# Two attention and two gated-unit layers on one core: the order of the work read from a table instead of a planner, and the first loads put on other queues

## The chip, the cores and the metric

The kernel runs on one core of a Trainium2 chip. The core has five engines with queues of their own: TensorE (PE, matrix products; the loads of its stationary operand are shown as PEld), VectorE (DVE), ScalarE (ACT), GpSimd (POOL) and SyncE (SP, which here only issues DMAs). ACT issues some DMAs too. Each engine takes its instructions strictly in the order of the program, and waits at an instruction until the semaphores it names have been set. Matmul results land in PSUM; DVE and ACT bring them to SBUF.

The metric is the device time of one execution in microseconds. Before the change the median of 3 runs is 382.63 us (381.41 to 382.69). The profiled execution took 380.91 us, and its span from the first to the last instruction is 379.2 us.

## The reference

The input is 2048 tokens of 512 numbers in bfloat16. Two kinds of layer alternate, twice: a linear attention A with 32 heads of 16, and a gated unit B of width 1376. Both layers A use the same weights, and so do both layers B.

```python
def _A_ref(x, wqkv, w_phi, wo):
    qkv = split into q, k, v of shape (1, 32, 2048, 16) from x @ wqkv
    pq = jnp.einsum("bhsd,hdf->bhsf", q, w_phi)
    pk = jnp.einsum("bhsd,hdf->bhsf", k, w_phi)
    phi_q = jnp.concatenate([_softmax(pq), _softmax(-pq)], axis=-1)
    phi_k = jnp.concatenate([_softmax(pk), _softmax(-pk)], axis=-1)
    kv = jnp.einsum("bhsf,bhsd->bhfd", phi_k, v)
    z  = jnp.einsum("bhsf->bhf", phi_k)
    num = jnp.einsum("bhqf,bhfd->bhqd", phi_q, kv)
    den = jnp.einsum("bhqf,bhf->bhq", phi_q, z)[..., None] + 1e-6
    return (num / den, heads joined) @ wo

def _B_ref(x, W_gate, W_up, W_down):
    gate, up = x @ W_gate, x @ W_up
    return (gate * (gate > 0) * up) @ W_down

x = x + _A_ref(_layernorm(x), ...)
x = x + _B_ref(_layernorm(x), ...)
x = x + _A_ref(_layernorm(x), ...)
x = x + _B_ref(_layernorm(x), ...)
```

## The kernel before, in words

The 2048 tokens are 16 tiles of 128, in four chunks of four. X stays in SBUF in bfloat16 all the time, and so do all weights, which are loaded once.

**Attention.** Each tile is normalised (`Norm.add`: batch-norm statistics `bnst` on DVE, the power -0.5 on POOL, the scaling on ACT or DVE), then turned so that the 512 features lie on the partitions, either by a DMA transpose on SP's queue or by PE with a copy out of PSUM. The key weights and w_phi are multiplied ahead into one matrix: `feature_weights` turns the key weights on PE (line 351), copies them (ACT or DVE), multiplies with the block form `Wblk` of w_phi (line 364) and copies the product to `Wk`; the same with the query weights to `Wq`. A tile's keys then take one matmul group (line 710), two exponentials on ACT (plus and minus, line 715), the sums of each head on DVE (lines 682 and 692; line 688 where POOL has added two halves, line 679), a reciprocal (724), and the scaling, split between DVE and POOL (730). The product with the values (line 663) is summed over all 16 tiles in PSUM (752). After the last tile `build_R` lays the sums out. Queries go the same way (lines 794, 798, 803 to 814), are turned by a DMA transpose (line 816), and multiplied with R (line 833, "er"). The quotient (851, 853) is turned (860, 866 or 873), multiplied with wo (884) and added to X (566). `Centre` subtracts the mean and turns the tile for the gated unit (524 to 542).

**Gated unit.** `glu` works by chunk, in parts of the chunk (`PARTS`), over ten blocks of 128 columns plus a rest of 96 (line 593). Gate and up products are matmuls with up to 512 tokens wide (613), ACT copies one of them (619, 623), DVE multiplies (626, 630). The down-projection (645) sums eleven blocks per tile; the result is scaled with the square of the norm's factor and added to X (570). In the second layer the tile is stored.

**The order.** Nothing is issued while these functions run: they record operations with an engine, a duration and what they read and write (`Plan.op`). `Plan.order` then plays the program through with these durations. At each moment an idle engine takes, of the operations whose inputs and buffers are there, the one with the highest sum of its longest path to the end and a number of its group (`RANK`); an operation of DVE marked `port` is not begun while a long one of POOL runs. The table `STEP` says for each tile which engine does a step. The resulting order is the order of the instructions on each engine, and also settles which buffer an operation gets. `load_weights` records 28 loads on SP (wo, the rests wr, wg, wu, wd), which the planner puts between SP's transposes. Ahead of all that `setup` issues the first loads: on SP the key weights, tiles 1, 2 and 3 of X and the value weights, on ACT tile 0, w_phi and the rest of X with the query weights. `wake` records matmuls on zeros, which are not used.

Of the kernel before, what the change touches and what calls it, by code (L numbers as in the profile page):

```python
# [8 lines left out]
P = 128  # L9
D = 512  # L10
# [3 lines left out]
NDB = D // P  # L14
# [36 lines left out]
TAIL = {"PE": 0.165, "ACT": 0.12, "DVE": 0.115, "POOL": 0.045, "SP": 0.0}  # L51
SAME = {"PE": -0.165, "ACT": 0.035, "DVE": 0.035, "POOL": 0.08, "SP": 0.0}
HOPS = {("DVE", "POOL"): 0.09, ("ACT", "POOL"): 0.15}
NEXT = {"PE": 0.055, "SP": 0.03}
FREE = 0.06


def hop(a, b):
    return SAME[a] if a == b else HOPS.get((a, b), NEXT.get(b, 0.04))


class Plan:
# [10 lines left out]
    def op(self, eng, occ, fn, reads=(), writes=(), holds=(), lat=0.0, at=0.0, group=None, port=False, long=False):  # L73

        o = Op()
        o.eng, o.occ, o.cost, o.fn, o.lat, o.at, o.port, o.long = eng, occ, occ + TAIL[eng], fn, lat, at, port, long
        o.group, o.i_in = group or self.group
        base, slope = RANK.get(f"{o.group}.{eng}") or RANK[o.group]
        o.bias = base - slope * o.i_in
        o.preds, o.succs, o.i = set(), [], len(self.ops)  # L80
# [18 lines left out]
    def order(self):  # L99
        for o in self.ops:  # L100
            for p in o.preds:
                p.succs.append(o)
        for o in reversed(self.ops):
            o.rank = o.cost + o.lat + max([s.rank + hop(o.eng, s.eng) for s in o.succs], default=0.0)
        free = {k: [0.0] * n for k, (pool, n) in self.kinds.items()}
        engines = sorted({o.eng for o in self.ops})
        busy = {e: 0.0 for e in engines}
        ready = {e: [] for e in engines}
        for o in self.ops:
            o.wait, o.t0 = len(o.preds), o.at  # L110
            if not o.wait:
                ready[o.eng].append(o)
        seq, left, now, shut = [], len(self.ops), 0.0, 0.0
        while left:
            moved, later = False, []
            for e in engines:
                if busy[e] > now + 1e-9:
                    later.append(busy[e])
                    continue
                best = None  # L120
                for o in ready[e]:
                    if o.t0 > now + 1e-9:
                        later.append(o.t0)
                        continue
                    if o.port and shut > now + 1e-9:
                        later.append(shut)
                        continue
                    ok = True
                    need = {}
                    for b in o.bufs:  # L130
                        if b.slot is None:
                            need[b.kind] = need.get(b.kind, 0) + 1
                    for k, n in need.items():
                        got = [t for t in free[k] if t is not None]
                        if len(got) < n:
                            ok = False
                        else:
                            t = sorted(got)[n - 1]
                            if t > now + 1e-9:
                                later.append(t)  # L140
                                ok = False
                    if ok and (best is None or (o.rank + o.bias, -o.i) > (best.rank + best.bias, -best.i)):
                        best = o
                if best is None:
                    continue
                o = best
                ready[e].remove(o)
                moved, left = True, left - 1
                o.start, end = now, now + o.cost
                busy[e] = now + o.occ  # L150
                if o.long:
                    shut = end
                later.append(busy[e])
                for b in o.bufs:
                    if b.slot is None:
                        b.slot = min((i for i, t in enumerate(free[b.kind]) if t is not None),
                                     key=lambda i: free[b.kind][i])
                        free[b.kind][b.slot] = None
                        b.end = 0.0
                    b.left -= 1  # L160
                    b.end = max(b.end, end + o.lat + FREE)
                    if not b.left:
                        free[b.kind][b.slot] = b.end
                for s in o.succs:
                    s.wait -= 1
                    s.t0 = max(s.t0, end + o.lat + hop(e, s.eng))
                    if not s.wait:
                        ready[s.eng].append(s)
                seq.append(o)
            if not moved:  # L170
                later = [t for t in later if t > now + 1e-9]
                assert later, "the plan is stuck"
                now = min(later)
        self.seq = seq
        return seq
# [15 lines left out]
WF_IN, WK_IN, WV_IN, WQ_IN, LOADED = 3.4, 4.2, 6.7, 10.4, 11.0  # L191
X_IN = [3.3, 4.5] + [5.2] * 2 + [7.4] * 4 + [8.9] * 4 + [11.8] * 4
# [8 lines left out]
def setup(ctx, tc, A_x, A_wqkv, A_w_phi, A_wo, B_W_gate, B_W_up, B_W_down, out):  # L201
# [35 lines left out]
    nc.scalar.dma_start(out=X[:, 4:8, :], in_=xv[:, 4:8, :])  # L237
    nc.scalar.dma_start(out=X[:, 8:12, :], in_=xv[:, 8:12, :])
    nc.scalar.dma_start(out=wq[:], in_=wv[:, :, 0:D])
    nc.scalar.dma_start(out=X[:, 12:16, :], in_=xv[:, 12:16, :])  # L240
# [53 lines left out]
def load_weights(st):  # L294

    nc, seen = st.nc, {}
    for n, (name, dst, src, kb) in enumerate(st.loads):
        i = seen[name] = seen.get(name, -1) + 1
        st.pl.rank("ld" if name == "wd" else "l", n)
        st.pl.op("SP", max(0.45, kb / 245.0), lambda dst=dst, src=src: nc.sync.dma_start(out=dst, in_=src), writes=[(name, i)], at=LOADED, lat=2.0)  # L300
# [11 lines left out]
def wake(st):  # L312

    nc, pl = st.nc, st.pl
    pl.rank("z")
    for i in range(STEP["wake"]):
        z = Buf("ps", [P, D], F32)
        pl.op("PE", 0.43 if i < 7 else 0.22, lambda z=z: nc.tensor.matmul(z[:], lhsT=st.zero[:, 0:P], rhs=st.zero[:], start=True, stop=True),
              writes=[(z, 0)], at=1.2)
# [689 lines left out]
```

## Time and profile before

| what | value |
|---|---|
| median of 3 runs | 382.63 us (381.41 to 382.69) |
| the profiled execution | 380.91 us, span 379.2 us |
| PE busy | 363.6 us (96%), 2380 matmuls |
| DVE busy | 268.0 us (71%) |
| ACT busy | 205.5 us (54%) |
| POOL busy | 121.1 us (32%) |
| DMA moved | 32.61 MB, mean 86 GB/s |
| chain that ended last, by engine | PE 64%, DVE 24%, DMA 6% |

The profile shows one execution. A row of a group names the source line, the engine, the operation, what is written and read, how often, the busy time and mean duration, and the idle time of the engine ahead of it with what ended it. Rows in order of time begin with the start and the length in us; "x4" says that four instructions in a row were merged. Matmuls overlap, so their single durations are longer than the distance from one to the next. Instructions that only issue a DMA are shown as SPq or ACTq and do not count as busy; the time a transfer takes runs from the issue to the landing, in the view of DMA issues. "PEclk" is the granted clock of PE.

### The profile page before, as it was taken

What the parts mean: (1) busy time and instruction counts of PE and PEld (TensorE: products, weight loads), DVE (VectorE), ACT (ScalarE), POOL (GpSimd) and SP (SyncE); (2) the same over time, 40 slices, a digit from 0 to 9 for tenths busy, and PEclk for the clock granted to TensorE, in tenths of its full rate; (3) what the DMA queues carried; (4) which work ended last, traced back from release to release, by engine and by line L of the source; (5) the groups of instructions that cost most, each with busy time, mean ns of one, the idle gap of its engine ahead of it and who ended that gap; (6) DMA issues with size and microseconds to landing.
All of it is one profiled execution on the core that took longest, in us unless ns stands there. A gap on an engine that the chain in (4) does not pass through costs nothing.

```text
span 379.2 us, 6724 instructions
## 1 busy us (share of the span) xinstructions
PE 363.6 (96%) x2380; PEld 189.9 (50%) x2409; DVE 268.0 (71%) x608; ACT 205.5 (54%) x439; POOL 121.1 (32%) x203
## 2 busy tenths in 40 slices
PE   4898999999899999999999999999999999999996
PEld 2444545756445444444444456475654445454444
DVE  4999999999925442763497998999962675172433
ACT  4898979776762446737706925865234135514100
POOL 3798965131110220560155681724310002000000
PEclk9999999999999999999999999999999999999999
DMA  8889936788950230021013070478930075000011
GB/s 262 239 143 227 260 44 144 133 149 146 145 107 2 42 58 15 0 30 27 0 22 77 9 119 3 87 127 146 171 85 14 5 146 115 14 0 16 1 55 57
DMA packets 98882, 32.61 MB, mean 86 GB/s; under 512 B 90560, under 2 KB 98336, under 8 KB 98848
## 3 DMA queue, kind: packets, MB, share of 16 engines
q1 hardware_dynamic: 97216, 29.93, 39.7%
q10 hardware_dynamic: 1632, 2.24, 1.8%
q8 instruction: 19, 0.31, 0.4%
q14 instruction: 15, 0.12, 0.1%
HBM read 8.44 MB, written 2.10 MB: 28 GB/s over the span
## 4 chain that ended last, share of the span: by engine, by line
PE 64%; DVE 24%; DMA 6%; issue 2%; ACT 1%; POOL 1%; SPq 0%; POOLq 0%; ACTq 0%
PE ps L613 37%; PE ps L645 14%; PE ps L884 5%; DMA b<-b 4%; DVE sk L682 4%; DVE rk L724 3%; DVE bnst L388 3%; PE ps L794 3%; PE ps L593 3%; DVE sk L692 2%; DVE b L730 2%; PE q L833 2%; DMA X<-in_A_x_dram 2%; DVE sq L682 1%; DVE sk L688 1%
## 5 line engine op out<-in xcount | busy, mean ns | idle before, releaser
L613 PE MATMUL ps<-b,wu 128*128 128x512 bf16 (+2 forms) x400 | 79.2, 336 | 0.6 <-DMA b<-b 0.6
L613 PE MATMUL ps<-b,wg 128*128 128x512 bf16 (+2 forms) x400 | 78.6, 336 | 0.0
L645 PE MATMUL ps<-wd,b 128*128 128x512 bf16 (+3 forms) x368 | 78.1, 366 | 0.3
L623 ACT ACTIVATE b<-ps 128x512 bf16<-128x512 f32 (+2 forms) x100 | 50.5, 520 | 39.6 <-PE ps L613 39.1
L626 DVE SCALAR_TENSOR_TENSOR b<-ps,b 128x512 bf16<-128x512 f32 (+2 forms) x60 | 35.1, 598 | 39.9 <-PE ps L613 38.9
L645 PEld LDWEIGHTS <-b 128*128 128x128 bf16 (+1 forms) x374 | 35.3, 98 | 39.1
L613 PEld LDWEIGHTS <-wg 128*128 128x128 bf16 x400 | 36.1, 98 | 33.1
L613 PEld LDWEIGHTS <-wu 128*128 128x128 bf16 x400 | 36.2, 98 | 32.7 <-issue 0.9
L730 POOL TENSOR_TENSOR b<-b,rk 128x1024 bf16<-128x1024 bf16 (+6 forms) x28 | 37.5, 1351 | 9.6 <-DVE rk L724 7.9
L798 ACT ACTIVATE b<-ps 128x512 bf16<-128x512 f32 x64 | 33.0, 638 | 5.7 <-PE ps L794 5.1
L715 ACT ACTIVATE b<-ps 128x512 bf16<-128x512 f32 x64 | 33.7, 628 | 1.3 <-PE ps L710 1.3
L679 POOL TENSOR_TENSOR b<-b 128x256 f32<-128x256 bf16 x30 | 19.7, 670 | 43.9 <-ACT b L715 34.1
L570 DVE SCALAR_TENSOR_TENSOR X<-ps,r,X 128x512 bf16<-128x512 f32 (+2 forms) x26 | 18.2, 701 | 20.2 <-PE ps L645 20.1
L710 PE MATMUL ps<-Wk,b 128*128 128x512 bf16 x123 | 29.4, 379 | 2.0 <-DMA b<-b 1.2
L884 PE MATMUL ps<-wo,b 128*128 128x512 bf16 x118 | 29.7, 379 | 1.5 <-DMA b<-b 0.9
L630 DVE TENSOR_TENSOR b<-b,b 128x512 bf16<-128x512 bf16 (+2 forms) x40 | 13.5, 348 | 24.0 <-ACT b L623 22.3
L552 POOL TENSOR_SCALAR ve<-tot 128x4 f32<-128x4 f32 x8 | 1.9, 233 | 88.8 <-ACT sq L548 88.8
L663 PE MATMUL ps<-wkv,b 128*128 128x512 bf16 x122 | 29.9, 386 | 0.3
L794 PE MATMUL ps<-Wq,b 128*128 128x512 bf16 x126 | 29.5, 379 | 0.1
L548 ACT ACTIVATE sq<-b 128x512 bf16<-128x512 bf16 x32 | 20.1, 627 | 17.4 <-DVE b L527 17.0
L598 ACT CAST ur<-ps 128x192 bf16<-128x192 f32 (+1 forms) x18 | 5.4, 302 | 32.2 <-PE ps L593 32.1
L814 POOL TENSOR_TENSOR b<-b,rq 128x512 bf16<-128x512 bf16 x19 | 20.2, 1061 | 8.4 <-DVE rq L807 6.1
(94 smaller groups left out, 493.7 us busy)
## 6 DMA issues: line engine op xcount, KB each, us to landing
out_dram<-X SPq DMA_DIRECT2D x15, 128.0 KB, 1.8
X<-in_A_x_dram ACTq DMA_DIRECT2D x3, 512.0 KB, 7.2
b<-b SPq DMA_TRANSPOSE x94, 3.2
wg<-in_B_W_gate_dram SPq DMA_DIRECT2D x8, 160.0 KB, 3.2
wu<-in_B_W_up_dram SPq DMA_DIRECT2D x8, 160.0 KB, 4.0
wd<-in_B_W_down_dram SPq DMA_DIRECT2D x5, 256.0 KB, 4.7
wkv<-in_A_wqkv_dram SPq DMA_DIRECT2D x2, 512.0 KB, 7.1
wq<-in_A_wqkv_dram ACTq DMA_DIRECT2D x1, 512.0 KB, 8.3
```

The source lines that it names most:

```text
L613: nc.tensor.matmul(ps[:], lhsT=wt[:, b, f * P:(f + 1) * P], rhs=xnT[:, lo:hi, b, :], start=(b == 0), stop=(b == NDB - 1))
L623: pl.op("ACT", 0.045 + 0.43 * share, lambda ups=ups, ru=ru, sign=1.0 if fuse else -1.0: nc.scalar.activation(out=ru[:], in_=ups[:], func=A ...
L626: pl.op("DVE", 0.06 + 0.548 * share, lambda gps=gps, ru=ru, h=h, cs=cs: nc.vector.scalar_tensor_tensor(out=h[:, cs], in0=gps[:], scalar=0. ...
L645: nc.tensor.matmul(yps[:], lhsT=hs[f][:fsz, ti * P:(ti + 1) * P], rhs=st.wd[:fsz, f, cols], start=(f == 0), stop=(f == NFT - 1))
L663: nc.tensor.matmul(vp[:], lhsT=xnT[:, ti, kb, :], rhs=st.wkv[:, kb, D:2 * D], start=(kb == 0), stop=(kb == NDB - 1))
L710: nc.tensor.matmul(ps[:], lhsT=xnT[:, ti, kb, :], rhs=w(kb), start=(kb == 0), stop=(kb == NDB - 1))
L715: pl.op("ACT", 0.48, lambda s=s, ek=ek, pk=pk: nc.scalar.activation(out=ek[:, :, s, :], in_=pk[:].rearrange("p (j x) -> p j x", j=8), func ...
L730: eng.tensor_tensor(out=phiK[:, lo:hi, :, :].rearrange("p j s (f h) -> p (j s) f h", h=4), in0=ek[:, lo:hi, :, :].rearrange("p j s (f h) - ...
L794: nc.tensor.matmul(pq[:], lhsT=xnT[:, ti, kb, :], rhs=st.Wq2[:, kb, :], start=(kb == 0), stop=(kb == NDB - 1))
L798: pl.op("ACT", 0.48, lambda s=s, eq=eq, pq=pq: nc.scalar.activation(out=eq[:, :, s, :], in_=pq[:].rearrange("p (j x) -> p j x", j=8), func ...
L814: (nc.vector if on_dve else nc.gpsimd).tensor_tensor(out=e, in0=e, in1=rq[:].unsqueeze(2).to_broadcast([P, 8, DH, 4]), op=Alu.mult)
L884: nc.tensor.matmul(yps[:], lhsT=turned(b), rhs=st.wo[:, b, :], start=(b == 0), stop=(b == NDB - 1))
```

## The change

The planner and the table RANK are gone. A table `ORDER` of 1867 numbers now says directly in which order the recorded operations are issued; `Plan.order` only hands out buffers, of those free at that place the one whose last use lies furthest back. STEP has new entries for almost every tile: which engine copies, sums and scales, which tiles are turned by PE. The first chunk of the first gated unit is cut into three parts (0 to 1, 1 to 2, 2 to 4) instead of two. No norm is made from sums any more (`sA` 0 instead of 2), and the gate that keeps the second layer's queries behind its key sums holds for the last chunk only (`gate` 3 instead of 1). 26 matmuls on zeros are recorded instead of 3, and the table puts them at places where PE has to wait at the start. An alternative path for the first keys (`raw`) is there and not used (`raw` is 0). The durations given with the operations are other ones in places, but nothing reads them now.

The first loads are issued from two lists: on SP tiles 0 and 1 of X and w_phi, on ACT the key weights first, then tiles 2 and 3, the value weights, and the rest, ahead of the load of ACT's function table.

```diff
     def order(self):
-        for o in self.ops:
-            for p in o.preds:
-                p.succs.append(o)
-        for o in reversed(self.ops):
-            o.rank = o.cost + o.lat + max([s.rank + hop(o.eng, s.eng) for s in o.succs], default=0.0)
...
+        owner = {k: [None] * n for k, (pool, n) in self.kinds.items()}
+        last = {k: [-1] * n for k, (pool, n) in self.kinds.items()}
+        assert sorted(ORDER) == list(range(len(self.ops)))
+        self.seq = [self.ops[i] for i in ORDER]
+        for at, o in enumerate(self.seq):
+            o.place = at
+            assert all(hasattr(p, "place") for p in o.preds), "an operation before what it needs"
+            for b in o.bufs:
+                if b.slot is None:
+                    free = [i for i, u in enumerate(owner[b.kind]) if u is None or not u.left]
+                    b.slot = min(free, key=lambda i: last[b.kind][i])
+                    owner[b.kind][b.slot] = b
+            for b in o.bufs:
+                b.left -= 1
+                last[b.kind][b.slot] = at
+        return self.seq
...
+LOAD_SP = ((0, 1), (1, 2), "f")
+LOAD_ACT = ("k", (2, 4), "v", (4, 8), (8, 12), "q", (12, 16))
...
-    nc.sync.dma_start(out=wkv[:, :, 0:D], in_=wv[:, :, D:2 * D])
-    nc.scalar.dma_start(out=X[:, 0:1, :], in_=xv[:, 0:1, :])
-    nc.scalar.dma_start(out=wf[:], in_=A_w_phi.rearrange("(b j) d f -> (j d) b f", b=NDB, j=8))
-    nc.sync.dma_start(out=X[:, 1:2, :], in_=xv[:, 1:2, :])
-    nc.sync.dma_start(out=X[:, 2:4, :], in_=xv[:, 2:4, :])
-    nc.sync.dma_start(out=wkv[:, :, D:2 * D], in_=wv[:, :, 2 * D:3 * D])
...
+    for what in LOAD_SP:
+        load(nc.sync, what)
+    for what in LOAD_ACT:
+        load(nc.scalar, what)
...
-    "part0": "4111", "part1": "6111", "tB0": "D---", "tB1": "--DA", "tA": "----", "wev": "ADADAAAAADDAAAAA",
+    "raw": 0, "kev": "ADAD", "part0": "3111", "part1": "6111", "tB0": "AD--", "tB1": "---A", "tA": "----",
+    "wev": "AAAAAAAADDDAAAAA", "xn1": "ADADDAADDAADAAAA", "turn": "-A--", "wake": 26, "fuse0": "AFAA",
...
+ORDER = [int(i) for i in """
+0 1 2 4 139 135 3 5 149 147 131 8 9 134 126 138 129 140 137 10 11 6 156 151 157 152 150 7 132 12 164 125 153 127 160
...
+""".split()]
```

What that does to the engines' instructions is shown at three places. In these rows, `b` with a number is a working tile, `ps` a PSUM tile, `wkv` the key and value weights, `X` the tokens.

ACT's first instructions, before:

```order
L226 DMA X<-in_A_x_dram 128x512
L227 DMA wf<-in_A_w_phi_dram 128x4x16
L236 ACT_TABLE_LOAD
L236 ACTIVATE wake<-zero 128x1
L237 DMA X<-in_A_x_dram 128x2048
L238 DMA X<-in_A_x_dram 128x2048
L239 DMA wq<-in_A_wqkv_dram 128x4x512
L240 DMA X<-in_A_x_dram 128x2048
L307 COPY b_130<-ps_131 128x512
L307 COPY b_139<-ps_140 128x512
```

And in the changed kernel:

```order
L161 DMA wkv<-in_A_wqkv_dram 128x4x512
L161 DMA X<-in_A_x_dram 128x1024
L161 DMA wkv<-in_A_wqkv_dram 128x4x512
L161 DMA X<-in_A_x_dram 128x2048 x2
L161 DMA wq<-in_A_wqkv_dram 128x4x512
L161 DMA X<-in_A_x_dram 128x2048
L170 ACT_TABLE_LOAD
L170 ACTIVATE wake<-zero 128x1
L390 ACTIVATE b_163<-X,ve_135,rstd_133 128x512
L237 COPY b_165<-ps_166 128x512
```

All of ACT's loads now stand ahead of the table load, the key weights are the first of them, and the first norm (line 390) is ahead of the copies of the turned key weights.

DVE at the start, from the first statistic to the fifth, before:

```order
L388 BN_STATS bnst_167<-X 128x6
L390 BN_AGGR mv_182<-bnst_154 128x2
L388 BN_STATS bnst_184<-X 128x6
L390 BN_AGGR mv_192<-bnst_167 128x2
L309 COPY b_148<-ps_149 128x512
L390 BN_AGGR mv_192<-bnst_184 128x2
L309 COPY b_160<-ps_161 128x512
L472 TENSOR_SCALAR b_205<-X,mv_182,rstd_190 128x512
L388 BN_STATS bnst_223<-X 128x6
```

And in the changed kernel:

```order
L402 TENSOR_SCALAR b_184<-X,mv_145,rstd_161 128x512
L318 BN_STATS bnst_211<-X 128x6
L318 BN_STATS bnst_220<-X 128x6
L320 BN_AGGR mv_222<-bnst_220 128x2
L320 BN_AGGR mv_222<-bnst_211 128x2
L318 BN_STATS bnst_225<-X 128x6
L318 BN_STATS bnst_227<-X 128x6
L402 TENSOR_SCALAR b_269<-X,mv_222,rstd_250 128x512
```

The two copies of turned key weights (line 309) have left DVE; the third to sixth statistics stand together, behind the norm of tile 1.

SP in the first attention, from the first turned query features (line 816) on, before:

```order
L816 DMA_TRANSPOSE b_949<-b_811 128x8x128
L816 DMA_TRANSPOSE b_963<-b_824 128x8x128
L816 DMA_TRANSPOSE b_999<-b_837 128x8x128
L816 DMA_TRANSPOSE b_1027<-b_846 128x8x128
L866 DMA_TRANSPOSE b_1059<-b_1042 128x4x128
L816 DMA_TRANSPOSE b_1108<-b_939 128x8x128
L816 DMA_TRANSPOSE b_1137<-b_953 128x8x128
L816 DMA_TRANSPOSE b_1152<-b_965 128x8x128
L816 DMA_TRANSPOSE b_1196<-b_980 128x8x128
L860 DMA_TRANSPOSE b_1243<-b_1150 128x8x128
```

And in the changed kernel, where line 762 is what line 816 was and line 230 what line 300 was:

```order
L762 DMA_TRANSPOSE b_949<-b_743 128x8x128
L230 DMA wu<-in_B_W_up_dram 128x640
L762 DMA_TRANSPOSE b_1011<-b_840 128x8x128
L762 DMA_TRANSPOSE b_1064<-b_733 128x8x128
L230 DMA wd<-in_B_W_down_dram 128x2x512
L762 DMA_TRANSPOSE b_1108<-b_909 128x8x128
L230 DMA wu<-in_B_W_up_dram 128x640
L230 DMA wd<-in_B_W_down_dram 128x2x512
L762 DMA_TRANSPOSE b_1214<-b_927 128x8x128
L806 DMA_TRANSPOSE b_1248<-b_1178 128x8x128
```

The last loads of the up and down weights, which stood ahead of all these transposes, now stand between them, and the next projection's transpose (line 806, before 860) comes after five turned query tiles instead of eight.

More of the change, by code (lines that the diff above doesn't have):

```diff
@@ L47 @@
     pass
[L51 to L59, printed above, removed]
 class Plan:
@@ L113, in order @@
[L113 to L173, printed above, removed]
@@ L317, in wake @@
         z = Buf("ps", [P, D], F32)
-        pl.op("PE", 0.43 if i < 7 else 0.22, lambda z=z: nc.tensor.matmul(z[:], lhsT=st.zero[:, 0:P], rhs=st.zero[:], start=True, stop=True),
+        pl.op("PE", 0.2155, lambda z=z: nc.tensor.matmul(z[:], lhsT=st.zero[:, 0:P], rhs=st.zero[:], start=True, stop=True),
               writes=[(z, 0)], at=1.2)
@@ L711, in mm, with raw, features @@
                                  start=(kb == 0), stop=(kb == NDB - 1))
-        pl.op("PE", 4 * MM, lambda pk=pk, mm=mm: mm(pk, lambda kb: st.Wk2[:, kb, :]),
-              reads=[(xnT, ti)] + [("Wk2", m) for m in range(NDB)], writes=[(pk, 0)], holds=(ek, phiK))
+        if L == "0" and t < STEP["raw"]:
+            kT, kTs = Buf("ps", [P, NDB, P], F32), Buf("b1", [P, NDB, P], BF16)
+            def raw(kT=kT, ti=ti):
+                for b in range(NDB):
+                    for kb in range(NDB):
+                        nc.tensor.matmul(kT[:, b, :], lhsT=st.wkv[:, kb, b * P:(b + 1) * P], rhs=xnT[:, ti, kb, :],
+                                         start=(kb == 0), stop=(kb == NDB - 1))
+            pl.op("PE", 16 * TR, raw, reads=[(xnT, ti)], writes=[(kT, 0)], holds=(kTs,), at=WK_IN)
+            evacuate(st, STEP["kev"][t], lambda kT=kT, kTs=kTs: (kTs[:], kT[:]), 0.59, reads=[(kT, 0)], writes=[(kTs, 0)])
+            def features(pk=pk, kTs=kTs):
+                for b in range(NDB):
+                    nc.tensor.matmul(pk[:, b * P:(b + 1) * P], lhsT=kTs[:, b, :], rhs=st.Wblk[:, b, :], start=True, stop=True)
+            pl.op("PE", 4 * TR, features, reads=[(kTs, 0), ("Wblk", 0), ("Wblk", 1)], writes=[(pk, 0)], holds=(ek, phiK))
+        else:
+            pl.op("PE", 4 * MM, lambda pk=pk, mm=mm: mm(pk, lambda kb: st.Wk2[:, kb, :]),
+                  reads=[(xnT, ti)] + [("Wk2", m) for m in range(NDB)], writes=[(pk, 0)], holds=(ek, phiK))
         for s in range(2):
```

78 lines of the change are left out of this document (31 added, 47 removed), and 103 rows, old and new, of tables (ORDER, RANK, STEP).

## Prediction

> **What bounds the kernel now.** I read the busy table by stage first, then the waits of TensorE (PE), then the start in order of time, then the issue of transposes on SyncE's queue (SP). The stages are cut at the fifth batch-norm statistic (10.6), PE's first gated-unit matmul (66.4), the end of a run of transposes (111.4), the second attention (204 to 275) and the end.
>
> ```profile
> core 0: us, PE busy (x) PEld busy (x) DVE busy (x) ACT busy (x) POOL busy (x), PEclk, DMA share, GB/s
> 0.00:10.60 10.60, 4.77 (x33) 3.24 (x34) 5.78 (x22) 4.33 (x7) 3.77 (x19) 1.00 0.84 273
> 10.60:66.40 55.80, 52.95 (x395) 27.01 (x401) 55.80 (x121) 50.31 (x98) 44.26 (x61) 1.00 0.76 173
> 66.40:111.40 45.00, 43.30 (x376) 26.66 (x379) 38.69 (x114) 33.03 (x90) 8.96 (x14) 1.00 0.80 140
> 111.40:204.00 92.60, 92.28 (x444) 43.14 (x449) 52.03 (x109) 45.12 (x89) 26.30 (x51) 1.00 0.13 25
> 204.00:275.00 71.00, 69.25 (x588) 40.30 (x592) 66.52 (x152) 43.71 (x98) 33.99 (x53) 1.00 0.54 94
> 275.00:379.20 104.20, 101.00 (x558) 49.59 (x560) 49.15 (x95) 29.00 (x59) 3.85 (x6) 1.00 0.20 46
> ```
>
> PE looks nearly full everywhere, but VectorE (DVE) is busy for the whole 55.80 us of the second row and 66.52 of 71.00 in the fifth: there PE keeps DVE's pace. To see what PE loses I count its work by width. The order has 1641 matmuls of 512 columns (shorter ones by their share, the zeros left out), the same in both kernels. A matmul of 512 columns in the steady stage takes 0.216 us:
>
> ```profile
> 13.63 0.60 PE L710 MATMUL ps<-Wk,b 128*128 128x512 bf16 x2
> 12.00 1.80 PE L663 MATMUL ps<-wkv,b 128*128 128x512 bf16 x4
> 66.44 0.49 PE L593 MATMUL ps<-wr,b 128*128 128x192 bf16 x4
> 127.36 0.82 PE L593 MATMUL ps<-wr,b 128*128 128x192 bf16 x8
> 220.47 1.89 PE L663 MATMUL ps<-wkv,b 128*128 128x512 bf16 x8
> 274.21 0.82 PE L593 MATMUL ps<-wr,b 128*128 128x192 bf16 x8
> ```
>
> (The L663 row of 220.47 has eight in 1.89, of which the last one's drain is 0.16: 0.216 each.) At 0.215 the 1641 are 352.9 us, so 26.3 of the 379.2 are lost. Ahead of the rows at 66.44, 127.36, 220.47 and 274.21 the order has work for 51.5, 108.8, about 201.5 and 251.8 us: lost so far 15.0, 18.5, 18.9 and 22.4. The rest, 3.9, is small losses and the last store. So the losses are 15.0 before the first gated unit, 3.5 up to 127, almost nothing in the long gated unit, and 3.5 in the second attention. The waits of PE that the profile names are few; its longest two (total us, times, longest):
>
> ```profile
> PE ps L351 <- DMA wkv<-in_A_wqkv_dram: 2.7, 1, 2.7
> PE ps L364 <- DVE b L309: 1.9, 1, 1.9
> ```
>
> **The start.** DVE's continuous run begins late:
>
> ```profile
> 3.86 0.69 DVE L388 BATCH_NORM_STATS2 bnst<-X 128x6 f32<-128x512 bf16 x1 [1.09 <-DMA X<-in_A_x_dram]
> 6.13 0.42 DVE L327 TENSOR_TENSOR Wblk<-M,wf 128x256 bf16<-128x256 bf16 x1 [1.32 <-DMA wf<-in_A_w_phi_dram]
> 8.25 0.69 DVE L388 BATCH_NORM_STATS2 bnst<-X 128x6 f32<-128x512 bf16 x1 [0.68 <-DMA X<-in_A_x_dram]
> 9.60 0.39 DVE L309 COPY b<-ps 128x512 bf16<-128x512 bf16 x1
> 10.62 0.69 DVE L388 BATCH_NORM_STATS2 bnst<-X 128x6 f32<-128x512 bf16 x1
> X<-in_A_x_dram SPq DMA_DIRECT2D x1, 256.0 KB, 6.4
> ```
>
> The third tile of X (256 KB, issued at 1.84 behind the key weights) lands at 8.2, and two copies of 0.39 come before the fifth statistic. In the changed kernel 1040 KB stand ahead of tiles 2 and 3 complete, and 2064 KB ahead of tiles 4 to 7. The first stage moved 273 x 10.6 = 2894 KB, all after about 2.0, so 337 KB a us: tiles 2 and 3 by 5.1, tiles 4 to 7 by 8.1, and up to a us for the notice (X's first 128 KB took 3.0 from issue, far more than its bytes). DVE's fifth statistic then starts near 9.05 (8.8 to 9.3) instead of 10.62, with the 0.6 of the two copies moved to ScalarE. Counted from zero work, DVE is ahead by 10.62 - 9.05 - 0.6, about 1.0; I take 0.6, since wf now lands third on SP's queue and its two products (0.35 each) wait for it. Ends: 0 and 1.6.
>
> On ScalarE seven issues now stand ahead of the table load. The sixth and seventh reuse the semaphores of X's first two tiles, as the issue of wq at 3.85 shows, just when X's first tile had landed (0.79 + 3.0). So the load (1.28) ends by about 6.3 instead of 3.0. The first activation needs the first tile's statistic and POOL's four small operations (6.74 to 8.18 before): about 6.0. Cost 0 to 0.3, behind DVE: 0.
>
> **The first attention, by DVE.** The order gives what DVE must have done when PE needs it, the by-form view and the rows above what each takes (starts lie 0.08 closer than the mean durations, as pieces overlap):
>
> ```profile
> L724 DVE RECIPROCAL rk<-sk 128x64 bf16<-128x64 f32 x32 | 16.6, 534 | 0.1
> L682 DVE TENSOR_REDUCE sk<-b 128x64 f32<-128x1024 bf16 x14 | 16.5, 1197 | 2.7 <-ACT b L715 2.7
> L388 DVE BATCH_NORM_STATS2 bnst<-X 128x6 f32<-128x512 bf16 x24 | 16.1, 678 | 1.9 <-DMA X<-in_A_x_dram 1.8
> L692 DVE TENSOR_REDUCE sk<-b 128x32 f32<-128x512 bf16 x23 | 14.8, 661 | 0.9 <-ACT b L715 0.9
> L688 DVE TENSOR_REDUCE sk<-b 128x32 f32<-128x256 f32 x13 | 7.4, 575 | 0.2 <-POOL b L679 0.2
> 74.31 2.54 PE L645 MATMUL ps<-wd,b 128*128 128x512 bf16 x11
> ```
>
> Before, 131 operations stand ahead of the first gated-unit matmul: 16 statistics with aggregates 10.8, 13 full sums 14.6, 14 half sums 8.3, 9 sums of POOL's halves 4.6, 24 reciprocals 9.4, the rest 12.8, together 60.5. It ran at 66.44, so DVE's clock stands at work + 5.9. Test: ahead of the first down-projection are 67.9, which gives 73.8; it ran at 74.31. After, 121 operations (55.8) stand ahead of the first gated-unit matmul: at work + 5.3 it runs at 61.1, against 49.7 us of PE work: lost 11.4, not 15.0. But the new order asks more of DVE soon after: ahead of the second down-projection stand 189 operations (20 sums of halves and 24 half sums among them), 78.8 us, hence 84.1, where PE has 68.4 of work: lost 15.7. Third down-projection: 100.6 + 5.3 = 105.9 against 92.5: 13.4, no bound. So the peak is 15.7, where the old order had 15.8 at its first down-projection: **the gain of the first gated unit is given back 20 us later, and this term is 0.1.**
>
> **From 66 to 127, by SP.** The old order loses 18.5 - 15.8 = 2.7 more. There SP issues transposes without a gap:
>
> ```profile
> 68.73 1.25 SPq L860 DMA_TRANSPOSE b<-b  x1
> 110.22 1.22 SPq L603 DMA_TRANSPOSE b<-hr  x1
> 77.57 1.04 PE L884 MATMUL ps<-wo,b 128*128 128x512 bf16 x4 [0.46 <-DMA b<-b]
> 104.23 1.02 PE L613 MATMUL ps<-b,wu 128*128 128x512 bf16 x4 [0.57 <-DMA b<-b]
> ```
>
> From the first of these rows to the end of the second, 30 transposes take 42.7 us, 1.42 each. Beside PE's work from 50 to 90 us the old table has 30 of them, the new one 23: 33 us of issue in 40. The queue then has room, and of the 2.7 I take back 2.2 (ends 0 and 2.7; what stays is the few waits above for data that comes late for DVE's sake).
>
> **The second attention.** Beside PE's work from 190 to 250 us the old order holds 55.8 us of DVE work by its own durations, the new one 49.2, since key and query sums of the first chunks moved into the gated unit, where DVE has 52.03 of 92.60. The loss there is 3.5 (18.9 to 22.4). It is partly DVE's pace and partly the chain from the last key through R and the transposes, which stays. I take 1.1, nearer the end that keeps the chain; ends 0 and 3.5.
>
> **What is added.** The first chunk of the gated unit in three parts instead of two, 80 matmuls more of the same total width: 80 x 0.0025 = 0.2 (the 0.216 of a row less 0.2133 for its columns, an estimate from the steady step). Twenty-six zero matmuls instead of three: twenty stand before PE's first real key matmul, where it waits for loads and copies anyway, six behind it; 6 x 0.216 = 1.3 if none is hidden, 0 taken, as DVE sets the pace there. POOL gains four scalings of 1.06 and seven half adds of 0.67, 8.9 us, and loses 4.4 in small ones, by the orders' counts. In the first attention, where it is busy 44.26 of 55.80, that may hold DVE, see the rivals; by itself it is beside DVE's work: 0. Weights' issues: 28 as before.
>
> Sum: -0.1 - 2.2 - 1.1 + 0.2 = -3.2: a span of 376.0. The profiled run took 380.91, 1.7 over its span: 377.7. The median of the runs is 382.63, 1.7 above that run, so on the scale of medians **379.4 us**, 0.8% faster. Own range of this case 377 to 381.
>
> **Rivals.**
> *More is won.* If PE's half-speed start sets the lag and not DVE, the zeros pay: before 13.63 PE's rows run at 0.45 a full width (1.80 for four) and after at 0.216, and its 3.0 us of real work (14 full widths) took 5.9. That would give 2.9 at the start in place of 0.1, hence 376.6. Against it: DVE's 55.80 of 55.80. [...]
>
> *The queue gives nothing.* If the transposes land late because their sources do, 23 issues instead of 30 change nothing, and with the second attention unmoved only 0.1 is left against 0.2 added: 382.7. For it: the wait rows above are only 0.46 and 0.57.
>
> *Weights come late.* The last up-projection block now stands behind four transposes of query features on SP, the fourth of which needs DVE's work up to PE's 46 us, near 59. It lands 4.0 after an issue near 60.5 (view of DMA issues), 64.5, and all of the first gated unit waits for it, where DVE would let it go at 61.1. The lag is then 14.8, below the peak of 15.7; it costs only if the issue slips by over 1 us. Priced at 1.5: 380.9.
>
> ```profile
> wu<-in_B_W_up_dram SPq DMA_DIRECT2D x8, 160.0 KB, 4.0
> 23.97 0.70 DVE L472 TENSOR_SCALAR b<-X,mv,rstd 128x512 bf16<-128x512 bf16 x1
> 22.82 1.70 POOL L730 TENSOR_TENSOR b<-b,rk 128x896 bf16<-128x896 bf16 x1
> 165.20 1.18 DVE L472 TENSOR_SCALAR b<-X,rstd,ve 128x512 bf16<-128x512 bf16 x1
> ```
>
> *Slower: DVE held by POOL.* The normalisation at 23.97 took 0.70 instead of its 0.41 and ended behind POOL's product (to 24.52); the one at 165.20 took 1.18. So a POOL operation can hold a DVE one, 0.3 to 0.8 us each time, and six such cases in the whole program cost 2.3. POOL's long work beside PE's 50 to 60 us rises from 1.4 to 6.5 us, just ahead of the second down-projection where DVE is the bound. At 0.55 each, nine more holds make +5: 15.7 becomes 20.7, over the 18.5 of today; that is +2.2 there, -1.1 in the second attention, +0.2 added: 383.9; with four holds in the second attention too, 386. It outweighs the forecast's gain from six holds on (3.2 / 0.55). [...] Against this rival: the table puts each such DVE operation by a rule that avoids running POOL work, as the old planner did with six misses.
>
> **Numbers.** Forecast 0.45; more is won 0.15; the queue gives nothing 0.14; weights late 0.06; slower 0.20. About 0.5%, 1.9 us, is what a measurement of this kernel can tell from no change. Faster by more than that: the first two, 0.60; within it 0.18 (0.12 of the third, and the fourth); slower 0.22, with the 0.02 left of the third. Range 375.6 to 386: from a us below the fast rival to the slow one.
>
> **What would show it.** Fifth statistic at 8.8 to 9.3; first gated-unit matmul near 61, second down-projection near 84; no gap-free run of 30 transposes; DVE below 66 of 71 us in the second attention; the row of zeros before the first key transpose at 0.43, then 0.22. Wrong if the loss at PE's 109 us of work is still 18, or if DVE's short SBUF operations take over half a us more often than six times.

## The result: 0.55% slower, in the first attention and at DVE

The changed kernel takes 383.88 us (median), the one before 382.07 in the same session: ratio 1.0055, 95% interval 1.0035 to 1.0075. The prediction said 379.4. The profiled run of the changed kernel took 384.54, 2.2 over its span.

The same stages as in the prediction, of the changed kernel:

```profile
core 0: us, PE busy (x) PEld busy (x) DVE busy (x) ACT busy (x) POOL busy (x), PEclk, DMA share, GB/s
10.60:66.40 55.80, 50.56 (x372) 25.92 (x378) 55.04 (x113) 46.51 (x90) 42.30 (x64) 0.97 0.73 160
66.40:111.40 45.00, 43.31 (x431) 30.86 (x437) 43.04 (x122) 34.09 (x106) 15.89 (x27) 1.00 0.73 122
204.00:275.00 71.00, 70.34 (x580) 39.90 (x589) 64.16 (x143) 44.66 (x101) 33.96 (x48) 1.00 0.39 70
```

DVE is still full in the first attention (55.04 of 55.80), PE does 2.4 us less there than before; in the second attention PE does 1.1 more. The waits of PE, and the rows of its first gated-unit matmul and second down-projection:

```profile
PE q L698 <- DVE b L676: 4.4, 3, 2.0
PE ps L543 <- DVE X L496: 1.1, 1, 1.1
69.01 0.39 PE L543 MATMUL ps<-b,wg 128*128 128x128 bf16 x4
89.12 1.70 PE L575 MATMUL ps<-wd,b 128*128 128x512 bf16 x7
```

The key sums (line 698) wait 4.4 us in three places for scalings of DVE (line 676); the kernel before has no such wait. I count the loss as the prediction did: the time of a matmul less the full-width matmuls ahead of it in the order, at 0.215 us each. In us, for PE's work so far, from the profiles of all kernels that the argument needs (to about 0.3, as some matmul records are missing; the lower rows are kernels of the section on experiments, and a hold is a DVE operation that POOL keeps waiting):

```
PE's work ahead               20    40    60    80   109   200   252   end
before                      13.4  14.2  15.8  16.9  18.6  19.2  22.5  26.4
changed                     11.6  17.4  20.7  22.6  22.7  23.4  25.3  29.4
before, three holds put in  14.0  17.5  19.8  21.6  22.1  22.8  25.9  31.1
three scalings ahead        13.7  17.7  20.1  22.0  22.1  22.8  25.7  29.9
all moves                   11.9  14.2  16.9  18.9  19.0  19.7  21.9  26.1
all moves, one hold back    11.9  15.3  18.0  20.0  20.1  20.8  23.2  27.4
all moves, 483 earlier      11.8  14.0  16.7  17.9  17.9  18.6  21.3  25.4
```

At 20 us of work the changed kernel is 1.8 ahead; by 40 it is 3.2 behind, by 80 5.7, at 109 and 200 about 4.2, and behind the second attention 2.8. (0.6 to 0.9 of the changed kernel's 3.3 between 40 and 60, by the 2.4 to 2.7 of the other kernels of its order in the table, goes with a stretch in which the granted clock was 0.50. By their mean clock only three of the eleven executions have one, the profiled one among them: last section.)

Where DVE loses it, in order of time, DVE's rows and POOL's beside them:

```profile
20.78 0.88 DVE L402 TENSOR_SCALAR b<-X,mv,rstd 128x512 bf16<-128x512 bf16 x1
34.44 2.48 POOL L676 TENSOR_TENSOR b<-b,rk 128x512 bf16<-128x512 bf16 x2
35.49 1.72 DVE L676 TENSOR_TENSOR b<-b,rk 128x512 bf16<-128x512 bf16 x1
41.88 3.35 POOL L676 TENSOR_TENSOR b<-b,rk 128x896 bf16<-128x896 bf16 x2 [2.55 <-DVE rk L670]
43.90 1.87 DVE L676 TENSOR_TENSOR b<-b,rk 128x1024 bf16<-128x1024 bf16 x1
55.48 1.86 DVE L676 TENSOR_TENSOR b<-b,rk 128x384 bf16<-128x384 bf16 x2
55.74 1.05 POOL L760 TENSOR_TENSOR b<-b,rq 128x512 bf16<-128x512 bf16 x1
95.91 1.05 POOL L760 TENSOR_TENSOR b<-b,rq 128x512 bf16<-128x512 bf16 x1
95.97 1.14 DVE L402 TENSOR_SCALAR b<-X,mv,rstd 128x512 bf16<-128x512 bf16 x1 [0.31 <-POOL rstd L328]
212.31 1.91 POOL L676 TENSOR_TENSOR b<-b,rk 128x1024 bf16<-128x1024 bf16 x1
212.44 1.93 DVE L402 TENSOR_SCALAR b<-X,mv,rstd 128x512 bf16<-128x512 bf16 x1
```

Each of these DVE operations begins with or in a POOL operation and ends 0.1 to 0.6 us behind it (beside the first, a half add of POOL runs to 21.52; the second piece of the 55.48 row begins at 55.80 and takes 1.54). Five in the first attention (the fifth, at 32.57, is 0.75 long instead of 0.23) take 4.4 us more than the same forms take alone; before, such excess was 0.6 in this stage. By form, changed kernel first, the kernel "all moves, 483 earlier" second (total, mean ns):

```profile
L402 DVE TENSOR_SCALAR b<-X,mv,rstd 128x512 bf16<-128x512 bf16 x17 | 10.0, 604 | 0.3 <-POOL rstd L328 0.3
L676 DVE TENSOR_TENSOR b<-b,rk 128x1024 bf16<-128x1024 bf16 x6 | 6.1, 1011 | 0.0
L622 DVE TENSOR_REDUCE sk<-b x26: 624/673/686, 19.0 to 232.0; 128x32 f32<-128x512 bf16 x26
```

```profile
L402 DVE TENSOR_SCALAR b<-X,mv,rstd 128x512 bf16<-128x512 bf16 x17 | 7.4, 452 | 0.5 <-POOL rstd L328 0.5
L676 DVE TENSOR_TENSOR b<-b,rk 128x1024 bf16<-128x1024 bf16 x6 | 4.4, 730 | 0.0
```

The key sums of line 622 (least, median, longest ns) never take longer than 686, though 21 of the 26 run beside a POOL operation of over half a us; the query sums of the same line stay below 710. The operations held in the rows above are the scalings of line 676 (up to 1.87) and the normalisations of line 402 (up to 1.93); these reduces were not held.

### The profile page after: what moved, and what is told of

The parts are those of the page before. It is cut to its first block, busy times and chain, and to the rows that moved or that the text cites. A ratio compares the mean times of both kernels' runs of the same rounds, so it can differ in the third digit from the quotient of the medians.

```text
span 382.3 us, 6828 instructions
## 1 busy us (share of the span) xinstructions
PE 367.9 (96%) x2474; PEld 196.3 (51%) x2512; DVE 276.1 (72%) x617; ACT 201.1 (53%) x450; POOL 123.6 (32%) x203
## 4 chain that ended last, share of the span: by engine, by line
PE 68%; DVE 5%; issue 1%; POOL 1%; ACT 0%; POOLq 0%
PE ps L543 33%; PE ps L575 16%; PE ps L830 5%; PE ps L740 4%; PE ps L640 3%; PE ps L523 2%; PE ps L593 2%; PE q L779 2%; PE q L698 1%; DVE b L402 1%; DVE X L500 1%; DVE bnst L318 1%; DVE sk L612 1%; DVE sk L622 0%; DVE rk L670 0%
## 5 line engine op out<-in xcount | busy, mean ns | idle before, releaser
L553 ACT ACTIVATE b<-ps 128x512 bf16<-128x512 f32 (+3 forms) x110 | 50.4, 491 | 71.9 <-PE ps L543 69.9
L543 PE MATMUL ps<-b,wu 128*128 128x512 bf16 (+3 forms) x440 | 81.4, 321 | 1.1 <-DVE X L496 1.1
L543 PE MATMUL ps<-b,wg 128*128 128x512 bf16 (+3 forms) x440 | 82.1, 321 | 0.0
L500 DVE SCALAR_TENSOR_TENSOR X<-ps,r,X 128x512 bf16<-128x512 f32 (+2 forms) x34 | 23.8, 710 | 34.8 <-PE ps L575 34.6
L661 ACT ACTIVATE b<-ps 128x512 bf16<-128x512 f32 x64 | 36.5, 648 | 14.9 <-PE ps L640 14.8
L676 POOL TENSOR_TENSOR b<-b,rk 128x1024 bf16<-128x1024 bf16 (+7 forms) x26 | 35.4, 1367 | 15.3 <-DVE rk L670 8.2
L744 ACT ACTIVATE b<-ps 128x512 bf16<-128x512 f32 x64 | 35.1, 637 | 9.5 <-PE ps L740 5.3
L609 POOL TENSOR_TENSOR b<-b 128x256 f32<-128x256 bf16 x37 | 24.9, 685 | 27.3 <-ACT b L744 16.2
L549 ACT ACTIVATE b<-ps 128x128 bf16<-128x128 f32 (+2 forms) x50 | 21.1, 439 | 9.2 <-PE ps L543 8.7
L326 POOL TENSOR_SCALAR ve<-mv 128x2 f32<-128x2 f32 (+1 forms) x19 | 4.5, 238 | 65.8 <-DVE mv L320 65.5
L496 DVE SCALAR_TENSOR_TENSOR X<-ps,X 128x512 bf16<-128x512 f32 x32 | 21.7, 681 | 3.4 <-PE ps L830 3.4
```

The source lines that it names most:

```text
L500: pl.op("DVE", 0.04 + 0.535 * (cols.stop - cols.start) / D, lambda: nc.vector.scalar_tensor_tensor(out=st.X[:, t, cols], in0=yps[:], scala ...
L543: nc.tensor.matmul(ps[:], lhsT=wt[:, b, f * P:(f + 1) * P], rhs=xnT[:, lo:hi, b, :], start=(b == 0), stop=(b == NDB - 1))
L553: pl.op("ACT", 0.045 + 0.43 * share, lambda ups=ups, ru=ru, sign=1.0 if fuse else -1.0: nc.scalar.activation(out=ru[:], in_=ups[:], func=A ...
L661: pl.op("ACT", 0.48, lambda s=s, ek=ek, pk=pk: nc.scalar.activation(out=ek[:, :, s, :], in_=pk[:].rearrange("p (j x) -> p j x", j=8), func ...
L676: eng.tensor_tensor(out=phiK[:, lo:hi, :, :].rearrange("p j s (f h) -> p (j s) f h", h=4), in0=ek[:, lo:hi, :, :].rearrange("p j s (f h) - ...
L744: pl.op("ACT", 0.48, lambda s=s, eq=eq, pq=pq: nc.scalar.activation(out=eq[:, :, s, :], in_=pq[:].rearrange("p (j x) -> p j x", j=8), func ...
```

## Experiments

My theory after the result: the rival "Slower: DVE held by POOL" is what happened, because DVE sets the pace where the holds lie. Against it: the holds fill time in which DVE would have waited anyway, and the loss comes from the loads or from the order's dependencies. All ratios are to the kernel before on the same chip.

**Holds put into the kernel before.** Nothing but three of DVE's scalings changes place.

```
-        for o in self.order():
+        for o in moved(self.order(), self.ops):
+def moved(seq, ops):
+    for i, behind in ((206, 227), (251, 249), (264, 231)):
+        seq.remove(ops[i])
+        seq.insert(seq.index(ops[behind]) + 1, ops[i])
+    return seq
```

> The kernel before with three scalings of DVE taken ahead to places where POOL is in the middle of a long scaling (28.89 to 30.58, 34.70 to 36.87, 38.24 to 40.12). If a hold lasts to the end of POOL's operation and DVE sets the pace: 1.1, 1.0 and 1.5 us, so about 3.5 more: 385.6, with the first gated-unit matmul near 70 instead of 66.4. If holds are hidden: 382.1 within 0.6. If holds cost only the 0.55 that the prediction took for one: 383.7.

Measured 385.97 against 381.77; ratio 1.0080 (1.0048 to 1.0111), that is 1.8 to 4.2 us more.

```profile
27.57 3.35 POOL L730 TENSOR_TENSOR b<-b,rk 128x896 bf16<-128x896 bf16 x2
29.73 1.74 DVE L730 TENSOR_TENSOR b<-b,rk 128x1024 bf16<-128x1024 bf16 x1
37.22 1.28 DVE L730 TENSOR_TENSOR b<-b,rk 128x768 bf16<-128x768 bf16 x1
40.59 2.19 DVE L730 TENSOR_TENSOR b<-b,rk 128x896 bf16<-128x896 bf16 x2
70.39 0.25 PE L593 MATMUL ps<-wr,b 128*128 128x192 bf16 x1
```

The three cost DVE 1.1, 0.8 and 1.5 (the last is a piece of 128x128, 0.21 alone, second in its row), and the first gated-unit matmul comes at 70.39 instead of 66.44. Three holds alone make the kernel before at least as slow as the changed one. That they are hidden is out; that one costs 0.55 is too little.

**Holds taken out of the changed kernel.** Three steps, each by moving operations in the table:

```
+for i, ahead_of in ((265, 311), (200, 311), (313, 231)):
+    ORDER.remove(i)
+    ORDER.insert(ORDER.index(ahead_of), i)
```

> The changed kernel with three scalings of DVE taken ahead in its order (265 and 200 ahead of the reciprocal 311, 313 ahead of the full sum 231), so that the one that took 1.72 us beside POOL's scaling of 35.45 runs while POOL does short half adds. If POOL's holds set the loss: DVE reaches 62 us about 2 to 3 us of work further on, the loss at the first gated-unit matmul falls from 19.5 to about 17, and the time from 383.9 to about 381.5. If the holds only fill time in which DVE would have waited for something else: 383.9 within 0.5, with new idle time on DVE.

383.28; 1.0019 (0.9998 to 1.0040): 1.4 us less than the changed kernel's 1.0055, not 2.4. The scaling of 1.72 came down to 0.89 (it is the second in the row of 33.75 and now runs beside short half adds), and PE's wait at line 698 from 4.4 to 2.8. The loss at the first gated-unit matmul is 18.9, not about 17, but this profile has a stretch at half clock in the head (0.50, last section) and begins 2.1 higher; from 20 to 60 us of work it loses 6.4, the changed kernel 9.1. The holds near 44 and 56 us are there to the same 0.01 us (1.88, and 1.53 within the third row):

```profile
33.75 1.25 DVE L676 TENSOR_TENSOR b<-b,rk 128x256 bf16<-128x256 bf16 x2
44.22 1.88 DVE L676 TENSOR_TENSOR b<-b,rk 128x1024 bf16<-128x1024 bf16 x1
55.80 1.86 DVE L676 TENSOR_TENSOR b<-b,rk 128x384 bf16<-128x384 bf16 x2
```

They do not hang on chance timing. DVE's own reciprocal releases POOL's long operation (the 41.88 row: POOL idle 2.55 until it), and DVE's next scaling stands a few operations behind, while POOL is still at it.

```
+for i, ahead_of in ((483, 826), (1125, 1222)):   # two scalings of POOL, earlier
...
```

> The changed kernel with two scalings of POOL taken ahead in POOL's order (the query scaling 483 ahead of the small operation 826, the key scaling 1125 ahead of 1222), so that neither is running when the normalisations of DVE at 96 and 212 us, each released by POOL, begin. If holds cost what DVE shows: the normalisations take 0.41 instead of 1.14 and 1.93, the step of the loss from 21.0 to 22.6 near PE's 78 us of work goes, and the time falls by 1.2 to 2 to about 382.2. If the work behind them waits for something else: 383.9 within 0.5.

384.42; 1.0057 (1.0035 to 1.0078): nothing. The two normalisations are free (line 402: mean 452 instead of 604), but the scaling 483 now holds a product of the gated unit, and PE waits for that one instead:

```profile
90.51 1.20 DVE L560 TENSOR_TENSOR b<-b,b 128x128 bf16<-128x128 bf16 x2
90.52 1.11 POOL L760 TENSOR_TENSOR b<-b,rq 128x512 bf16<-128x512 bf16 x1
PE ps L575 <- DVE b L560: 0.7, 1, 0.7
```

Moving a hold is not removing it. Nor need every hold cost something: the longest one, at 212 us, went without a successor, and between 200 and 252 us of work the loss grows by 1.9 with it (23.4 to 25.3, changed kernel) and by 1.9 without it (24.6 to 26.5, this one). DVE has 6.8 of 71 us to spare there. Then all of these moves and two more:

```
+for i, ahead_of in ((265, 311), (200, 311), (313, 231), (321, 255),
+                    (323, 373), (346, 373), (356, 373), (483, 826), (1125, 1222)):
...
```

> All moves of the two kernels above and two more in the first attention: the full sum 321 ahead of the scaling 255 (held 1.2 us at 43.9), and the scalings 323, 346 and 356 ahead of the reciprocal 373, whose result lets POOL's query scaling go (held 0.9 at 55.8). If the holds are the loss: no DVE operation over 0.5 us too long in the first attention, DVE 3 to 4 us further at 62 us than in the changed kernel, time 380 to 381. If the first attention waits for something behind the holds: 382.5 to 383.5.

380.93; 0.9964 (0.9945 to 0.9982): 0.9% below the changed kernel and faster than the kernel before. PE's wait for the scalings is gone but for 0.9:

```profile
PE q L698 <- DVE b L676: 0.9, 2, 0.7
PE ps L575 <- DVE b L560: 0.7, 1, 0.7
85.55 1.20 DVE L560 TENSOR_TENSOR b<-b,b 128x128 bf16<-128x128 bf16 x2
```

With (321, 255) left out of the list, one hold comes back:

> The kernel with all moves, less one: the full sum 321 again behind the scaling 255. One hold, near 44 us, comes back. If a hold costs the whole kernel what DVE shows of it: 0.9 to 1.2 more than the kernel with all moves, so about 382. If only several together reach the end: no change within 0.4.

382.11; 0.9993 (0.9973 to 1.0012): 1.1 more. The loss is 1.1 higher from 40 us of work on and 1.3 at the end; the hold itself is 1.2 on DVE. PE's wait for the scalings grows with it, from 0.9 to 2.0:

```profile
PE q L698 <- DVE b L676: 2.0, 2, 1.4
```

Here one hold costs the whole kernel what DVE shows of it. It is also not the place of the scalings in the order by itself: in the kernel before, bringing three of them forward into POOL's operations made it slower. Last, with (482, 500) and (483, 500) in place of (483, 826):

> The kernel with all moves, but the query scaling 483 and the small product 482 ahead of it go further forward in POOL's order, ahead of the small product 500: where 483 stood, it held a product of the gated unit (row of L560, 1.07 us instead of 0.22) for which TensorE waited. If that hold is what the stage from 66 to 109 us of work loses: the two waits there (0.86 and 0.59 in the profile of the kernel with all moves) go, and the time falls by 0.6 to 1.4 to about 380. If the stage is bound by SP's queue or by DVE's plain work: no change within 0.4.

380.06; 0.9946 (0.9925 to 0.9967): 0.5% faster than the kernel before. The wait for line 560 is gone and the stage from 60 to 109 us of work loses 1.2 instead of 2.1. This version beats both kernels.

**The loads.** The old issue order in the changed kernel, and the new one in the kernel before:

```
-LOAD_SP = ((0, 1), (1, 2), "f")
-LOAD_ACT = ("k", (2, 4), "v", (4, 8), (8, 12), "q", (12, 16))
+LOAD_SP = ("k", (1, 2), (2, 4), "v")
+LOAD_ACT = ((0, 1), "f", (4, 8), (8, 12), "q", (12, 16))   # the last four behind the table load
...
```

> The changed kernel with the loads issued as before the change. If the new lists cost DVE time at the start (it waits 1.5 us for w_phi): DVE is ahead by 0.6 us at 11 us and the time is 383.3, give or take 1.5, since every later meeting of DVE and POOL shifts. If the new lists help, as the prediction said: 384.5 to 385.5.

> The kernel before with the new load lists alone, its order of instructions unchanged. If the lists cost DVE time: its fifth statistic starts later than 10.62 less what ScalarE now copies, and the time is 382.7 to 383.7 against 382.1. If they help as the prediction said: 380.5 to 381.5.

384.44, 1.0062 (1.0041 to 1.0083): no gain. And 383.72, 1.0028 (1.0006 to 1.0051): 1.1 us more. The first rows of DVE's feature weights in the two, and in the changed kernel:

```profile
7.08 0.76 DVE L257 TENSOR_TENSOR Wblk<-M,wf 128x256 bf16<-128x256 bf16 x2
```

```profile
7.75 0.43 DVE L327 TENSOR_TENSOR Wblk<-M,wf 128x256 bf16<-128x256 bf16 x1 [2.90 <-DMA wf<-in_A_w_phi_dram]
```

```profile
8.13 0.76 DVE L257 TENSOR_TENSOR Wblk<-M,wf 128x256 bf16<-128x256 bf16 x2 [1.54 <-DMA wf<-in_A_w_phi_dram]
10.61 1.25 DVE L318 BATCH_NORM_STATS2 bnst<-X 128x6 f32<-128x512 bf16 x2
```

In these profiles the new lists cost DVE 0.8 in either order, waiting for w_phi (the fifth statistic starts at 10.61 instead of 9.79, and at 11.45 instead of 10.62). With the holds gone the comparison was made again:

> The same with the loads issued as before the change. If DVE's start still counts once the holds are gone: 0.6 to 0.8 below the kernel above, so near 379.7. If what DVE gains at the start is lost again in the second attention, as the loads alone suggest: the same as the kernel above within 0.4.

381.80; 0.9995 (0.9972 to 1.0018): here the old lists are 1.2 slower than the new ones by the ratios, 0.9 by the medians. DVE's start gains nothing in this profile: w_phi comes early (6.97 instead of 7.90), but DVE then waits 0.7 for the third tile of X, and the fifth statistic starts at 10.48 instead of 10.41. So no price of the lists by themselves shows: the new ones gain 1.2 with this order and cost 1.1 with the old one. Three of the twelve executions with the old lists and all moves ran at a mean clock of 0.994 to 0.996, none of those with the new lists below 0.998; the other nine have a median of 381.47, so about half of the difference goes with the clock. What makes the rest stays open.

**The zeros.** All but 3 of the 26 left out; in the changed kernel, then in the one with all moves:

```
-        pl.op("PE", 0.2155, lambda z=z: nc.tensor.matmul(z[:], ...
+        pl.op("PE", 0.2155, (lambda: None) if 3 <= i else lambda z=z: nc.tensor.matmul(z[:], ...
```

> The changed kernel with only the first three of its 26 zero matmuls (no result depends on them). As the prediction had it (zeros lie beside waits): 383.9 within 0.5. If they keep TensorE's clock up: the first key matmuls take 0.43 instead of 0.22 and the time is 385 to 386.8. If the six behind the first key matmul stand in the way: 382.6.

> The kernel with all moves and three zero matmuls instead of 26 (no result depends on them). If the zeros are worth the 1.3 to 1.8 that their removal cost in the changed kernel: about 382.5. If that was late transposes and not the zeros: the same as the kernel with all moves within 0.5. If they guard the clock: some executions with a granted clock below 0.997, where the kernel with all moves has none.

385.73, 1.0089 (1.0060 to 1.0119), and 383.15, 1.0030 (1.0012 to 1.0049): 1.3 and 2.5 us more than with the zeros. Yet the loss at 20 us of work is the same (11.7 against 11.6, 12.0 against 11.9), and the mean clock is 0.998 to 1 in every execution of the second. Two more kernels keep only the three late ones of those 23, or leave just these out (`i not in (0, 1, 2, 18, 21, 24)`, `i in (18, 21, 24)` as the condition):

> The kernel with all moves; of its 26 zero matmuls the 20 that stand up to 17 us are left out but for three, the three later ones stay (33, 53 and 61 us in its profile). No result depends on them. If the early zeros are worth the 2.2 us that all of them are: 383.1. If the late ones are: 380.9 within 0.5.

> The kernel with all moves without the three zero matmuls at 33, 53 and 61 us; the 23 up to 17 us stay. No result depends on them. If the early zeros are worth the 2.2 us: 380.9 within 0.5. If the late ones are, by keeping PE busy just ahead of its waits: about 383.

382.04, 1.0001 (0.9984 to 1.0018), and 381.55, 0.9997 (0.9979 to 1.0014): about half each. Without the late ones the profile loses 0.8 more between 50 and 55 us of work, at rows that wait for transposes. Without the early ones the profiled run is as fast as with them (379.0 against 378.9), while the executions spread from 380.7 to 383.9 instead of 380.6 to 381.4. What the zeros do is not settled.

## Why the prediction was wrong

**The step that failed is POOL's added work, "by itself it is beside DVE's work: 0".** It was about 3.8 us of DVE's time in the first attention (4.4 of holds, 0.6 before). With it falls the sentence set against the rival, that the table avoids running POOL work by a rule; that was read from the names in the code, and the order on record shows POOL's scalings released by the reciprocal just ahead of DVE's. The rival gave 383.9, and that is the time; its mechanism was right, its sizes were not: not nine holds of 0.55 but five of 0.5 to 1.3, since each lasted until POOL ended (the DVE operations end 0.1 to 0.6 us behind it). Its place was not right either: the five lie at 20 to 57 us, ahead of PE's 40 us of work, and not beside PE's 50 to 60, where the rival counted POOL's new work. That the same time came out is in part luck. I priced by the short holds of before (0.3 to 0.8 us) instead of by POOL's durations, though the one at 23.97 had ended behind POOL's 1.70 already.

*The start.* The fifth statistic was to begin at 9.05; it begins at 10.61, behind 1.54 us of waiting for w_phi. Against the same operations' durations DVE stood 6.3 behind its work in the kernel before at 12 us and stands 7.0 behind in the changed one. Mis-sized by 1.3: 0.7 lost where 0.6 was to be won.

*First attention by DVE.* The rule, DVE's work plus its lag, was right; the lag was 10.7 instead of 5.3. The second down-projection was to need 78.8 us of DVE's work, so 89.5: it ran at 89.12. In the last version the lag is 6.7 and the row comes at 85.11, loss 16.8 where 15.7 was forecast. The first gated-unit matmul was too early even so (61.1 forecast, 69.01, 65.01 in the last version): PE stands behind other rows there, which I had not followed.

*From 66 to 127 by SP.* PE's named waits for transposed tiles at the projection, the rest and the gated unit fell from 0.9, 0.6 and 0.6 to none, as forecast (in the last version 0.9 stands at the projection again), but the hold at 95.97 took part of their place (PE's wait of 1.1 at line 543). Between 60 and 109 us of work the stage loses 2.0 instead of 2.8; in the last version, without that hold, 1.2. So 0.8 was won, and 1.6 could be, of the 2.2 forecast.

*Second attention.* DVE 64.16, below 66; loss 1.9 instead of 3.3: 1.4 won, 1.1 forecast. Right; with less lag ahead of it, in the last version, it is only 0.6.

*What is added.* The zeros were put at 0, and removing them costs 1.3 to 2.5 us; the price of the rival with PE's half-speed start was nearer, but not its cause: in the changed kernel PE leaves half speed early (the eleven leading zeros start 0.42 apart, the one at 6.51 us takes 0.22 to the next start; before, the four full widths from 12.00 on still start 0.41 apart), but the head loses the same with three zeros as with 26 (11.7 against 11.6 at 20 us of work). This share of the change helped the changed kernel, and nothing in my sum had it. The 0.2 for 80 matmuls more is borne out by the profile of before: 80 matmuls of 512 columns take 17.27 us from 166.86 on, 24 of 128 columns 1.34 from 67.81 on, which leaves 0.0024 a matmul beside its columns.

The signs named beforehand were there: the loss at 109 us of work is 22.7, not under 18, and seven short operations of DVE take over half a us too long. The other rivals are out: PE waits for no weights, and the transposes' relief did come.

With the long holds of the first attention out the kernel takes 380.06, near the 379.4 of the forecast, but by partly cancelling errors: start and second attention worse, zeros better.

## What to carry to other kernels

Before work is moved to POOL, list what DVE does in the 1 to 2 us behind each event that releases a POOL operation: if a scaling, a normalisation or a product of two SBUF tiles stands there, it may wait for POOL's end, as it did here (a normalisation took 1.93 us instead of 0.41, a product of the gated unit 1.07 instead of 0.22); put reduces, reciprocals or operations from PSUM there. The key sums of line 622 never took longer than 0.69 here. In the changed kernel 16 of 32 reciprocals (line 670) and 13 of 32 sums out of PSUM (line 496) ran beside a POOL operation of over half a us, and none took longer than 0.55 and 0.69 us, where the rest reach 0.55 and 0.71. Price a hold by POOL's remaining time, and when one is moved, look at what it now meets. Where DVE was full, a hold passed to the end (1.1 us for one of 1.2 on DVE); where it had time to spare (6.8 of 71 us), the one at 212 us cost nothing.

## What the runs showed of the hardware that was not expected

In some profiles PE's granted clock falls to half for 3.4 us in the middle of the work. In the changed kernel it is 0.50 from 57.44 to 60.84 us, behind the waits for the held scalings (1.57 and 0.85 us):

```profile
54.00:57.80 3.80, 1.39 (x33) 1.22 (x33) 3.80 (x9) 1.62 (x4) 1.62 (x2) 0.95 0.44 81
57.80:61.20 3.40, 3.18 (x17) 1.35 (x16) 2.94 (x7) 1.38 (x3) 2.14 (x4) 0.55 0.83 116
61.20:64.00 2.80, 2.80 (x32) 1.61 (x29) 2.50 (x7) 2.34 (x6) 2.22 (x4) 1.00 0.80 185
```

In the kernel with three scalings ahead it falls to 0.50 in the head (first two rows), where the kernel with all moves, no busier just before, keeps the full clock of 1.00 (last two):

```profile
8.00:11.00 3.00, 1.61 (x22) 1.28 (x22) 2.96 (x9) 3.00 (x8) 0.32 (x2) 0.99 1.03 408
11.00:14.40 3.40, 3.18 (x13) 1.48 (x12) 3.40 (x10) 2.35 (x6) 2.60 (x7) 0.50 1.15 323
8.00:11.00 3.00, 1.59 (x22) 1.26 (x22) 2.96 (x8) 3.00 (x7) 0.36 (x2) 1.00 1.04 410
11.00:14.40 3.40, 3.35 (x21) 1.45 (x18) 3.40 (x10) 3.40 (x8) 2.56 (x7) 1.00 1.17 303
```

By the mean clock only some executions of a kernel have such a stretch: of the changed kernel three (0.994 to 0.995) of eleven, the others stand at 0.998 to 1. PE does, by an estimate, about 1.6 us less of its work in it (half of the 3.18 us for which it is busy), but the price to the kernel is not fixed. Divided by their mean clock (below 0.997, and the others), the executions of the changed kernel have medians of 384.44 and 383.84 (3 and 8 of them), those of the kernel with three scalings ahead 383.70 and 382.34 (7 and 5), and those of the kernel before, measured beside it, 381.70 and 381.90 (8 and 21): 0.6 us, 1.4 us and nothing. Why only some executions meet it, no run here shows.

The hold also reaches pieces that are short by themselves: a 128x128 scaling of 0.21 us took 1.7 beside a POOL scaling of 1.88.
